# Local attention fused with two gated layers: the global queries' PV product issued inside the local PV block

## The chip, the cores and the metric

One core of one Trainium2 chip runs the whole program. The metric is device time in microseconds of one execution, the median of several.

## The reference

Attention with a local window and a few global tokens, then two token-wise layers. Batch 4, 8 heads of width 64, 32 global and 512 local tokens per batch, all in float32:

```python
k_all, v_all = concat([k_g, k_l]), concat([v_g, v_l])
out_g = softmax(scale * q_g @ k_all.T) @ v_all           # 32 global queries see all 544 keys
s_ll  = where(|i - j| <= 32, scale * q_l @ k_l.T, -1e9)
s_lg  = scale * q_l @ k_g.T
out_l = softmax(concat([s_lg, s_ll])) @ v_all            # local queries: window and global keys
x = concat([out_g, out_l]) as 2176 tokens x 512
x = rmsnorm(x) * rms_g
x = (silu(x @ w_gate) * (x @ w_val)) @ w_out             # first layer, width 1536
x = (s * relu(x @ w_in)**2 + b) @ w_out2                 # second layer, width 2048
```

## The kernel before, in words

The 2176 tokens go through the two layers in five groups: the local tokens of batches 0, 1 and 2 (512 each), and two groups of 320 with the halves of batch 3 and the global tokens. A group takes 12 slots of the first layer and 16 of the second. In a slot `emit_first` forms a 128-wide slice of hidden units in a PSUM bank `m` (two buffers), ACT and DVE apply the gate or the square, and `emit_second` adds the slice's product to four accumulators `acc` one slot later. Every product is three matmuls (lines 622, 623, 624), since each operand is split into a rounded part and a rest (`hl`, line 140: a cast on ACT or DVE, then a subtraction on DVE, line 142). Here they are called the large matmuls. In the first group the weights are also read from their raw form and converted on ACT and DVE (`conv`, lines 171 to 192); later groups load the converted ones.

The attention of the next group runs between the large matmuls. A unit is one batch and one pair of heads; `unit_steps` (line 290) gives its steps, `unit_queue` (line 410) strings those of four units together, and `tick` emits the next step when a modelled time allows: the distance is the step's lag or the time left divided by the steps left, whichever is longer, at most 4 us. The framework then orders each engine's instructions itself by a simulation, so a different queue changes the order of much besides the edit.

Steps of a unit with local queries: scores and their row maxima (`sc`, DVE line 281), exponentials (`st_e`, ACT line 331), reciprocals (`st_r`), scaling (`st_n`), transposes (`st_t`, PE lines 253 and 254, copied to SBUF on ACT line 257), and the local PV (`st_v`, line 386): `values` issues 16 matmuls on line 268 and 8 with the global keys on line 276, then DVE copies the result `u` (line 138) and the loads of the next unit are issued. All attention matmuls use one PSUM tile `at` of two banks with one buffer.

Odd units (`kp`) also do the global queries of their own and the preceding unit: scores (`st_g`, lines 318 and 319), one exponential, transposes (`st_tg`, lines 357 and 359, copied into `pgt`) and `st_gv`: 20 matmuls on line 377 into an `at` tile of their own, copied by DVE to `xg` (line 379). The trace counts each float32 matmul twice, as two passes. Six units have local queries and are odd; two more odd units have global queries only.

At the end of a group's second layer `build_steps` (line 444) makes the next group's input `x`: squares on ACT (455), a sum over partitions on PE (470), a logarithm and an exponential on ACT (474, 475, each with a table load), four DVE steps (476 to 479), and per slice a scaling (487) and a split into `x`.

Of the kernel before, what the change touches and what calls it, by code (L numbers as in the profile page):

```python
# [19 lines left out]
SG, SL = 32, 512  # L20
# [5 lines left out]
VW = 9 * 128 + 64  # L26
# [37 lines left out]
def attn_moe_kernel(ctx: ExitStack, tc: tile.TileContext, s0, q, k, v, w1, w2, cst, out):  # L64
# [27 lines left out]
    V, A, G, PE = nc.vector, nc.scalar, nc.gpsimd, nc.tensor  # L92

    def banks(tag):
        return ps.tile([128, 2, 512], F32, tag=tag, name=tag)
# [6 lines left out]
    def in_turn(mms):  # L102
        for a, b in zip(mms, mms[1:]):
            tc.add_manual_dep(b.ins, a.ins.name, behind, reason="in turn")
# [29 lines left out]
    def cpy(e, out_, in_):  # L134
        if e == "A":
            A.copy(out=out_, in_=in_)  # L136
        else:
            V.tensor_copy(out=out_, in_=in_)
# [68 lines left out]
    def u_tile(b):  # L207
        if b not in ut:
            ut[b] = u_p.tile([128, HP, 4, 128], F32, tag="u", name="u")
        return ut[b]  # L210

    def xg_tile(b):
        if b not in xg_t:
            xg_t[b] = xg_p.tile([128, HP, SG], F32, tag=f"xg{b}", name="xg")
        return xg_t[b]

    def load_u(i):
        if i >= len(UNITS) or i in raw_u:
            return
        b, p, loc = UNITS[i]  # L220
        vr = at_p.tile([128, VW], F32, tag="vr", name="vr", bufs=2)
        e = ST if loc else SG
        qr = at_p.tile([128, ST], F32, tag="qr", name="fq")
        kr = kr_p.tile([128, 8, KW], F32, tag="kr", name="fk")
        nc.sync.dma_start(out=qr[:, 0:e], in_=q[b, p, :, 0:e])
        nc.sync.dma_start(out=kr, in_=k[b, p])
        nc.sync.dma_start(out=vr, in_=v[b, p])
        raw_u[i] = (qr, kr, vr)
# [28 lines left out]
        A.copy(out=t.rearrange("p a n -> p (a n)"), in_=flat[:, 0:640])  # L257
        return t

    def values(bk, vr, vg, pts):  # L260
        mms = []
        for c in range(2 * len(pts)):
            t = pts[c // 2]
            for e in range(2):
                for h in range(2):
                    i = 2 * c + e
                    o = 128 * (c // 2) + 64 * e
                    mms.append(PE.matmul(bk[64 * h:64 * h + 64, c % 2, o:o + 64],  # L268
                                         lhsT=vr[:, 128 * i + 64 * h:128 * i + 64 * h + 64],
                                         rhs=t[:, 2 * (c % 2) + h, 64 * e:64 * e + 64], start=(c < 2 and e == 0), stop=False))  # L270
        for c in range(2 * len(pts)):
            t = pts[c // 2]
            for h in range(2):
                x = slice(32 * (2 * (c % 2) + h), 32 * (2 * (c % 2) + h) + 32)
                o = 128 * (c // 2)
                mms.append(PE.matmul(bk[64 * h:64 * h + 64, c % 2, o:o + 128], lhsT=vg[x], rhs=t[x, 4],
                                     start=False, stop=(c // 2 == len(pts) - 1), tile_position=(x.start, 64 * h)))
        in_turn(mms)
# [11 lines left out]
    def unit_steps(i):  # L290
        b, p, loc = UNITS[i]
        S = {}
        kp = p % 2
# [70 lines left out]
            A.copy(out=tv[:, 1:5], in_=bk[:, 1].rearrange("p (a n) -> p a n", a=4))  # L364
            S["pgt"] = t

        def st_gv():
            bk = banks("at")[:, 0]
            t = S["pgt"]
            mms = []  # L370
            for e in range(2):
                vr = raw_u[i - 1 + e][2]
                for a in range(5):
                    for h in range(2):
                        o = bk[64 * h:64 * h + 64, SG * e:SG * e + SG]
                        w = 128 * min(2 * a, 8) + 64 * h
                        mms.append(PE.matmul(o, lhsT=vr[:, w:w + 64], rhs=t[:, a, e, h], start=(a == 0), stop=(a == 4)))  # L377
            in_turn(mms)
            V.tensor_copy(out=xg_tile(b)[:, p - 1:p + 1], in_=bk[:, 0:2 * SG].rearrange("p (e n) -> p e n", e=2))
            if not loc:  # L380
                load_u(i + 1)

        def st_t(c0):
            S["pt", c0] = transposes(banks("at"), pm[:, c0:c0 + 2], S["gl", c0])

        def st_v():
            bk = banks("at")
            vr = raw_u[i][2]
            values(bk, vr, vr[:, VW - 64:VW], [S["pt", 0], S["pt", 2]])
            cpy("V", u_tile(b)[:, p].rearrange("p (c b) n -> p c b n", b=2),  # L390
                bk[:, :, 0:256].rearrange("p b (c n) -> p c b n", c=2))
            load_u(i + 1)

        if not loc:
# [7 lines left out]
            se=[(lambda: st_e((0, 1), False), 1.0)] + ([(st_g, 0.8)] if kp else [])  # L402
            + [(lambda: st_e((2, 3), kp == 1), 1.0)],
            rn=[(st_r, 1.0), (lambda: st_n(0), 0.3), (lambda: st_n(1), 0.3)]
            + ([(st_tg, 1.5), (st_gv, 1.0)] if kp else []),
            tv=[[(lambda: st_t(0), 1.0), (lambda: (st_n(2), st_n(3)), 1.0), (lambda: st_t(2), 1.0)]],
            pv=[[(st_v, 1.5)]])

# [255 lines left out]
    for n, (ph, gi, f) in enumerate(slots):  # L664
# [13 lines left out]
        w = wt[n]  # L678
        if ph == 1:
# [9 lines left out]
            h = act_p.tile([128, 2, NMAX], F32R, tag="h", name="h")  # L689
            a = tmp_p.tile([128, NMAX], F32, tag="ta", name="a")  # L690
# [8 lines left out]
        else:  # L699
# [7 lines left out]
            t = tmp_p.tile([128, NMAX], F32, tag="ta", name="t")  # L707
            h = act_p.tile([128, 2, NMAX], F32R, tag="h", name="h2")
# [93 lines left out]
```

## Time and profile before

| | |
|---|---|
| median of 3 runs | 996.24 us (994.8 to 998.65) |
| the profiled execution | 997.97 us |
| its span | 995.6 us |
| PE busy | 946.3 us, 95% of the span |
| DVE, ACT busy | 471.7 us, 464.9 us |
| mean granted TensorE clock | 0.972 of full speed |

The span runs from the first to the last instruction on the core. PE's busy time counts overlapping matmuls once, so gaps between its rows are what is left. A matmul's row is longer than the distance to the next one, since matmuls are pipelined; the cost of a stretch is read from the starts of its rows.

### The profile page before, as it was taken

What the parts mean: (1) busy time and instruction counts of PE and PEld (TensorE: products, weight loads), DVE (VectorE), ACT (ScalarE), POOL (GpSimd) and SP (SyncE); (2) the same over time, 40 slices, a digit from 0 to 9 for tenths busy, and PEclk for the clock granted to TensorE, in tenths of its full rate; (3) what the DMA queues carried; (4) which work ended last, traced back from release to release, by engine and by line L of the source; (5) the groups of instructions that cost most, each with busy time, mean ns of one, the idle gap of its engine ahead of it and who ended that gap; (6) DMA issues with size and microseconds to landing.
All of it is one profiled execution on the core that took longest, in us unless ns stands there. A gap on an engine that the chain in (4) does not pass through costs nothing.

```text
span 995.6 us, 15191 instructions
## 1 busy us (share of the span) xinstructions
PE 946.3 (95%) x6024; PEld 790.7 (79%) x6024; DVE 471.7 (47%) x1149; ACT 464.9 (47%) x908; POOL 0.8 (0%) x9
## 2 busy tenths in 40 slices
PE   5758999889999999999999999999999999999998
PEld 4437777667877778777877878778789999999998
DVE  6995978769954141334353131443442243421322
ACT  5886697667744152533346252633441342311222
POOL 0000000000000000000000000000000000000000
PEclk9578999999999999999999999999999999999999
DMA  9985789848964754446565655346488848988584
GB/s 371 409 324 204 282 306 349 308 162 311 356 240 170 264 203 183 163 143 225 213 232 191 239 204 187 142 173 245 167 308 337 305 159 309 340 338 300 181 328 153
DMA packets 41110, 249.54 MB, mean 251 GB/s; under 512 B 5072, under 2 KB 6096, under 8 KB 23120
## 3 DMA queue, kind: packets, MB, share of 16 engines
q1 hardware_dynamic: 41040, 248.58, 67.4%
q8 instruction: 47, 0.77, 0.3%
q14 instruction: 23, 0.19, 0.0%
HBM read 208.46 MB, written 40.11 MB: 250 GB/s over the span
## 4 chain that ended last, share of the span: by engine, by line
PE 80%; DMA 7%; DVE 6%; ACT 5%; issue 1%; SPq 0%; ACTq 0%; DVEq 0%
PE m L622 15%; PE m L624 14%; PE m L623 14%; PE acc L622 10%; PE acc L623 10%; PE acc L624 10%; DMA wr<-in_w_dram 4%; DMA wt<-wsc 2%; PE at L237 2%; PE at L268 1%; ACT ce L177 1%; PE at L377 1%; PE at L253 1%; DVE wt L142 1%; DMA fq<-in_q_dram 1%
## 5 line engine op out<-in xcount | busy, mean ns | idle before, releaser
L623 PE MATMUL acc<-h,wt 128*128 128x512 f32 (+1 forms) x560 | 200.6, 359 | 1.4 <-DVE h L142 1.3
L624 PE MATMUL acc<-h,wt 128*128 128x512 f32 (+1 forms) x560 | 200.2, 358 | 0.0
L622 PE MATMUL acc<-h,wt 128*128 128x512 f32 (+1 forms) x560 | 192.5, 363 | 0.5 <-DVE y L142 0.3
L622 PE MATMUL m<-x,wt 128*128 128x512 f32 (+2 forms) x496 | 178.7, 362 | 11.3 <-ACT x L136 9.2
L623 PE MATMUL m<-x,wt 128*128 128x512 f32 (+2 forms) x496 | 175.8, 355 | 0.1
L624 PE MATMUL m<-x,wt 128*128 128x512 f32 (+2 forms) x496 | 175.3, 354 | 0.0
L622 PE MATMUL m<-y,wt 128*128 128x512 f32 (+1 forms) x320 | 117.0, 373 | 7.6 <-DVE t L711 4.2
L623 PE MATMUL m<-y,wt 128*128 128x512 f32 (+1 forms) x320 | 116.2, 364 | 2.9 <-DVE y L142 2.9
L623 PEld LDWEIGHTS acc<-h,wt 128*128 128x128 f32 x560 | 105.2, 188 | 15.3 <-DVE h L142 2.1
L622 PEld LDWEIGHTS acc<-h,wt 128*128 128x128 f32 x560 | 103.6, 188 | 16.3 <-issue 1.7
L624 PEld LDWEIGHTS acc<-h,wt 128*128 128x128 f32 x560 | 105.1, 188 | 13.6 <-issue 0.5
L624 PE MATMUL m<-y,wt 128*128 128x512 f32 (+1 forms) x320 | 115.4, 361 | 0.0
L622 PEld LDWEIGHTS m<-x,wt 128*128 128x128 f32 x496 | 93.9, 190 | 26.4 <-ACT x L136 9.9
L692 DVE TENSOR_TENSOR a<-sg,m 128x512 f32<-128x512 f32 (+1 forms) x60 | 36.4, 607 | 142.9 <-PE m L624 136.5
L624 PEld LDWEIGHTS m<-x,wt 128*128 128x128 f32 x496 | 93.9, 189 | 11.1 <-issue 0.3
L623 PEld LDWEIGHTS m<-x,wt 128*128 128x128 f32 x496 | 93.9, 189 | 10.8 <-DVE x L142 0.8
L711 DVE SCALAR_TENSOR_TENSOR t<-m,ct,r 128x512 f32<-128x512 f32 (+1 forms) x80 | 53.2, 670 | 98.3 <-ACT r L710 98.1
L710 ACT ACTIVATE r<-m 128x512 f32<-128x512 f32 (+1 forms) x80 | 42.1, 532 | 115.2 <-PE m L624 115.0
L685 ACT ACTIVATE sg<-m 128x512 f32<-128x512 f32 (+1 forms) x60 | 32.0, 534 | 96.9 <-PE m L624 96.7
L136 ACT CAST h<-a 128x512 fp32r<-128x512 f32 (+1 forms) x60 | 33.3, 555 | 92.2 <-DVE a L692 73.2
L622 PEld LDWEIGHTS m<-y,wt 128*128 128x128 f32 x320 | 59.8, 189 | 20.8 <-ACT y L136 4.4
L713 ACT ACTIVATE h<-t,ct 128x512 fp32r<-128x512 f32 (+1 forms) x80 | 52.2, 658 | 50.9 <-DVE t L711 33.1
(141 smaller groups left out, 1137.6 us busy)
## 6 DMA issues: line engine op xcount, KB each, us to landing
wt<-wsc SPq DMA_DIRECT2D x48, 1536.0 KB, 7.5
wt<-wsc SPq DMA_DIRECT2D x64, 1024.0 KB, 4.8
wr<-in_w_dram SPq DMA_DIRECT2D x68, 512.0 KB, 6.3
wsc<-wt SPq DMA_DIRECT2D x12, 1536.0 KB, 7.3
wsc<-wt SPq DMA_DIRECT2D x16, 1024.0 KB, 6.2
fk<-in_k_dram SPq DMA_DIRECT2D x16, 640.0 KB, 5.3
vr<-in_v_dram SPq DMA_DIRECT2D x16, 608.0 KB, 6.0
s_w<-in_s_dram SPq DMA_DIRECT2D x8, 736.0 KB, 11.5
```

Of the source, the lines that this page charges most:

```text
L136: A.copy(out=out_, in_=in_)
L142: V.tensor_tensor(out=dst_l, in0=src, in1=dst_h.bitcast(F32), op=ALU.subtract)
L177: A.copy(out=e.bitcast(I16), in_=odd)
L237: mms.append(PE.matmul(bk[64 * e:64 * e + 64, h, n * KW:(n + 1) * KW], lhsT=qr[x, q0 + 64 * i:q0 + 64 * i + 64], rhs=kr[x, i]))
L622: PE.matmul(out_, lhsT=wh, rhs=xh, start=first, stop=False)
L623: PE.matmul(out_, lhsT=wh, rhs=xl, start=False, stop=False)
L624: PE.matmul(out_, lhsT=wl, rhs=xh, start=False, stop=last)
L685: A.activation(out=sg[:, :N], in_=gb[:, :N], func=AF.Silu)
L692: V.tensor_tensor(out=a[:, :N], in0=sg[:, :N], in1=vb[:, :N], op=ALU.mult)
L710: A.activation(out=r[:, :N], in_=hb[:, :N], func=AF.Relu)
L711: V.scalar_tensor_tensor(out=t[:, :N], in0=hb[:, :N], scalar=ct[:, C_S:C_S + 1], in1=r[:, :N], op0=ALU.mult, op1=ALU.mult)
L713: A.activation(out=h[:, 0, :N], in_=t[:, :N], func=AF.Identity, bias=ct[:, C_B:C_B + 1])
```

## The change

For odd units with local queries the step `st_gv` is gone from the queue. Its 20 matmuls are made by `gv_mms` and handed to `values`, which issues them between its matmuls with the local values (line 268) and those with the global keys. They write columns 256 to 319 of the first `at` bank, which the local PV leaves free, without start or stop flags. `gv_copy` then takes them to `xg`, ahead of the copy to `u`. Units with global queries only keep `st_gv`.

```diff
--- before.py
+++ after.py
@@ -257,7 +257,7 @@
         A.copy(out=t.rearrange("p a n -> p (a n)"), in_=flat[:, 0:640])
         return t
 
-    def values(bk, vr, vg, pts):
+    def values(bk, vr, vg, pts, more=None):
         mms = []
         for c in range(2 * len(pts)):
             t = pts[c // 2]
@@ -268,6 +268,8 @@
                     mms.append(PE.matmul(bk[64 * h:64 * h + 64, c % 2, o:o + 64],
                                          lhsT=vr[:, 128 * i + 64 * h:128 * i + 64 * h + 64],
                                          rhs=t[:, 2 * (c % 2) + h, 64 * e:64 * e + 64], start=(c < 2 and e == 0), stop=False))
+        if more:
+            mms += more()
         for c in range(2 * len(pts)):
             t = pts[c // 2]
             for h in range(2):
@@ -364,8 +366,7 @@
             A.copy(out=tv[:, 1:5], in_=bk[:, 1].rearrange("p (a n) -> p a n", a=4))
             S["pgt"] = t
 
-        def st_gv():
-            bk = banks("at")[:, 0]
+        def gv_mms(bk, fresh):
             t = S["pgt"]
             mms = []
             for e in range(2):
@@ -374,11 +375,18 @@
                     for h in range(2):
                         o = bk[64 * h:64 * h + 64, SG * e:SG * e + SG]
                         w = 128 * min(2 * a, 8) + 64 * h
-                        mms.append(PE.matmul(o, lhsT=vr[:, w:w + 64], rhs=t[:, a, e, h], start=(a == 0), stop=(a == 4)))
-            in_turn(mms)
+                        mms.append(PE.matmul(o, lhsT=vr[:, w:w + 64], rhs=t[:, a, e, h], start=(fresh and a == 0),
+                                             stop=(fresh and a == 4)))
+            return mms
+
+        def gv_copy(bk):
             V.tensor_copy(out=xg_tile(b)[:, p - 1:p + 1], in_=bk[:, 0:2 * SG].rearrange("p (e n) -> p e n", e=2))
-            if not loc:
-                load_u(i + 1)
+
+        def st_gv():
+            bk = banks("at")[:, 0]
+            in_turn(gv_mms(bk, True))
+            gv_copy(bk)
+            load_u(i + 1)
 
         def st_t(c0):
             S["pt", c0] = transposes(banks("at"), pm[:, c0:c0 + 2], S["gl", c0])
@@ -386,7 +394,10 @@
         def st_v():
             bk = banks("at")
             vr = raw_u[i][2]
-            values(bk, vr, vr[:, VW - 64:VW], [S["pt", 0], S["pt", 2]])
+            gk = bk[:, 0, 256:256 + 2 * SG]
+            values(bk, vr, vr[:, VW - 64:VW], [S["pt", 0], S["pt", 2]], (lambda: gv_mms(gk, False)) if kp else None)
+            if kp:
+                gv_copy(gk)
             cpy("V", u_tile(b)[:, p].rearrange("p (c b) n -> p c b n", b=2),
                 bk[:, :, 0:256].rearrange("p b (c n) -> p c b n", c=2))
             load_u(i + 1)
@@ -402,7 +413,7 @@
             se=[(lambda: st_e((0, 1), False), 1.0)] + ([(st_g, 0.8)] if kp else [])
             + [(lambda: st_e((2, 3), kp == 1), 1.0)],
             rn=[(st_r, 1.0), (lambda: st_n(0), 0.3), (lambda: st_n(1), 0.3)]
-            + ([(st_tg, 1.5), (st_gv, 1.0)] if kp else []),
+            + ([(st_tg, 1.5)] if kp else []),
             tv=[[(lambda: st_t(0), 1.0), (lambda: (st_n(2), st_n(3)), 1.0), (lambda: st_t(2), 1.0)]],
             pv=[[(st_v, 1.5)]])
```

**First place: PE, second unit of batch 1, in the first layer of the first token group.** Before, the global PV (377, 20 matmuls) and the local PV (268 and 276) are two blocks.

```order
L624 MATMUL acc_873<-h,wt 128x512
L377 MATMUL at<-pgt,vr 64x32 x20
L622 MATMUL m<-x,wt 128x512
...
L624 MATMUL acc_873<-h,wt 128x512
L268 MATMUL at<-ptf,vr 64x64 x16
L276 MATMUL at<-ptf,vr 64x128 x8
L622 MATMUL acc_872<-h,wt 128x512
```

Now (line numbers of the changed file: 378 is the global PV, 278 the old 276, 633 to 635 the old 622 to 624):

```order
L635 MATMUL m<-x,wt 128x512
L268 MATMUL at<-ptf,vr 64x64 x16
L378 MATMUL at<-pgt,vr 64x32 x20
L278 MATMUL at<-ptf,vr 64x128 x8
L633 MATMUL m<-x,wt 128x512
```

The 20 matmuls moved from a place of their own into the block of the local PV; all six units of this kind show the same.

**Second place: DVE, where the first group goes from its first to its second layer.** `y` is the second layer's input, in four slices of which the last two are in the rows; `qf` takes the next unit's global queries out of a load; `t` frees a bank for the second layer. `cv` and `wt` rows are weight conversion. Before:

```order
L142 TENSOR_TENSOR y<-acc_872,y 128x512
...
L187 SCALAR_TENSOR_TENSOR cv<-wr,cv 128x1024
L340 TENSOR_SCALAR rs<-sum 128x8
L300 COPY qf<-fq 64x32 x2
L189 SCALAR_TENSOR_TENSOR cv<-wr,cv 128x1024
L341 RECIPROCAL rs<-rs 128x8
L142 TENSOR_TENSOR y<-acc_873,y 128x512
L142 TENSOR_TENSOR wt<-cv,wt 128x2x512
...
L711 SCALAR_TENSOR_TENSOR t<-m,ct,r 128x512 x2
```

Now (line 722 is the old 711):

```order
L142 TENSOR_TENSOR y<-acc_872,y 128x512
L142 TENSOR_TENSOR y<-acc_873,y 128x512
L302 COPY qf<-fq 64x32 x2
L142 TENSOR_TENSOR wt<-cv,wt 128x2x512
L184 TENSOR_SCALAR cv<-cv 128x1024
L185 TENSOR_SCALAR cv<-cv 128x1024
L342 TENSOR_SCALAR rs<-sum 128x8
L187 SCALAR_TENSOR_TENSOR cv<-wr,cv 128x1024
L343 RECIPROCAL rs<-rs 128x8
L178 TENSOR_SCALAR cv<-cv 128x1024
L189 SCALAR_TENSOR_TENSOR cv<-wr,cv 128x1024
L722 SCALAR_TENSOR_TENSOR t<-m,ct,r 128x512
```

The last `y` moved ahead of `qf` and of a conversion; the first `t` now stands behind `qf`, the end of one conversion (142) and five steps of others (184, 185, 187, 178, 189).

**Third place: PE and DVE, where the first group gives way to the second.** Before, on PE, 15 large matmuls stand between the sum (470) and the next unit's first scores (237):

```order
L624 MATMUL acc_1926<-h_2625,wt 128x512
L470 MATMUL at<-ss,ones 128x512
L622 MATMUL acc_1926<-h_2625,wt 128x512
...
L624 MATMUL m<-y,wt 128x512
L237 MATMUL at<-fk,fq 64x160 x8
L622 MATMUL m<-y,wt 128x512
```

Now (481 is the old 470):

```order
L634 MATMUL m<-y,wt 128x512
L635 MATMUL m<-y,wt 128x512
L481 MATMUL at<-ss,ones 128x512
L237 MATMUL at<-fk,fq 64x160 x16
L633 MATMUL m<-y,wt 128x512
```

The sum now has no large matmul behind it, and both score blocks (16 matmuls) follow at once. On DVE, before, from the last step of the root (479) on:

```order
L479 SCALAR_TENSOR_TENSOR r_2654<-nt,r_2654 128x512
L487 SCALAR_TENSOR_TENSOR xn<-u,ct,r_2654 128x512
L711 SCALAR_TENSOR_TENSOR t<-m,ct,r 128x512
L281 ISA pm,nm<-at,ct 128x160
L281 ISA nm 128x1
```

Now (490 is the old 479, 498 the old 487, 283 the old 281):

```order
L490 SCALAR_TENSOR_TENSOR r_2652<-nt,r_2652 128x512
L283 ISA pm,nm<-at,ct 128x160
L283 ISA nm 128x1
...
L283 ISA pm,nm<-at,ct 128x160
L283 ISA nm 128x1
L498 SCALAR_TENSOR_TENSOR xn<-u,ct,r_2652 128x512
L722 SCALAR_TENSOR_TENSOR t<-m,ct,r 128x512
```

Four row maxima moved ahead of `xn` and `t`. On ACT a relu of the second `m` bank (710) moved ahead of the logarithm's table load (474). `t` frees the `m` bank that PE's next large matmul writes. The last local PV of batch 1 stands 29 large matmuls ahead of the sum before, and 22 now.

## Rows read from the trace of the kernel before

**Rows 1.** The page: busy time by engine, and the granted TensorE clock in 40 slices.
```profile
PE 946.3 (95%) x6024; PEld 790.7 (79%) x6024; DVE 471.7 (47%) x1149; ACT 464.9 (47%) x908; POOL 0.8 (0%) x9
...
PEclk9578999999999999999999999999999999999999
```

**Rows 2.** Timeline of PE around one global PV block (start us, us, instructions).
```profile
165.18 0.39 PE L624 MATMUL acc<-h,wt 128*128 128x512 f32 x1
...
165.86 0.39 PE L624 MATMUL acc<-h,wt 128*128 128x512 f32 x1
166.18 1.36 PE L377 MATMUL at<-pgt,vr 128*64 128x32 f32 x40
167.47 0.50 PE L622 MATMUL m<-x,wt 128*128 128x512 f32 x1
167.80 0.39 PE L623 MATMUL m<-x,wt 128*128 128x512 f32 x1
```

**Rows 3.** Groups by line on PE: count, busy us, mean ns, idle before.
```profile
L377 PE MATMUL at<-pgt,vr 128*64 128x32 f32 x320 | 11.6, 224 | 0.0
```

**Rows 4.** Instructions of line 379: duration ns min/median/max.
```profile
L379 DVE COPY xg<-at x8: 218/224/225, 170.1 to 808.1; 128x64 f32<-128x64 f32 x8
```

**Rows 5.** Timeline, first to second product of the first token group.
```profile
189.57 0.69 DVE L138 COPY u<-at 128x512 f32<-128x512 f32 x1
...
189.69 1.90 ACT L177 COPY ce<-wr 128x2048 int16<-128x2048 int16 x1 [2.57 <-DVE wt L142]
...
191.49 0.58 ACT L136 CAST y<-acc 128x512 fp32r<-128x512 f32 x1
...
196.73 1.28 ACT L331 ACT_TABLE_LOAD   x1
...
197.18 0.69 DVE L184 TENSOR_SCALAR cv<-cv 128x1024 f32<-128x1024 f32 x1
...
198.03 0.43 ACT L331 ACTIVATE pm<-pm,n 128x160 f32<-128x160 f32 x1
...
199.18 1.23 DVE L187 SCALAR_TENSOR_TENSOR cv<-wr,cv 128x1024 int32<-128x1024 int32 x1
...
202.45 0.37 DVE L300 COPY qf<-fq 64x32 f32<-64x32 f32 x2 [0.81 <-DMA fq<-in_q_dram]
...
204.10 0.64 DVE L142 TENSOR_TENSOR y<-acc,y 128x512 fp32r<-128x512 f32 x1
...
206.97 0.75 DVE L711 SCALAR_TENSOR_TENSOR t<-m,ct,r 128x512 f32<-128x512 f32 x1
```

**Rows 6.** Timeline, first to second token group.
```profile
279.96 0.50 PE L623 MATMUL acc<-h,wt 128*128 128x512 f32 x1
...
286.67 1.02 PE L470 MATMUL at<-ss,ones 128*128 128x512 f32 x2
...
287.73 0.69 ACT L474 ACTIVATE r<-at,epsc 128x512 f32<-128x512 f32 x1 [0.95 <-PE at L470]
...
288.44 1.28 ACT L475 ACT_TABLE_LOAD   x1
...
291.17 0.60 ACT L710 ACTIVATE r<-m 128x512 f32<-128x512 f32 x1 [0.81 <-PE m L624]
...
293.25 0.75 DVE L711 SCALAR_TENSOR_TENSOR t<-m,ct,r 128x512 f32<-128x512 f32 x1
...
293.91 0.32 DVE L281 CUSTOM_DVE_ANT_0 pm<-at,ct 128x160 f32<-128x160 f32 x1
...
294.14 0.66 PE L622 MATMUL m<-y,wt 128*128 128x512 f32 x1 [2.30 <-DVE t L711]
...
303.00 0.50 PE L622 MATMUL m<-x,wt 128*128 128x512 f32 x1 [0.64 <-DVE t L711]
```

**Rows 7.** Busy time by stretch: us, then PE, PEld, DVE, ACT, POOL busy (count), granted clock, DMA share, GB/s.
```profile
293.00:299.00 6.00, 4.86 (x14) 3.70 (x14) 4.62 (x15) 3.35 (x11) 0.00 (x0) 0.72 0.13 55
```

**Rows 8.** The page: DMA issues, KB each, median us from issue to landing.
```profile
vr<-in_v_dram SPq DMA_DIRECT2D x16, 608.0 KB, 6.0
```

## Prediction, made before the changed kernel was run

> **What bounds the kernel now.** I read the page first. PE is busy for 95% of the span and its granted clock is at 9 tenths or more from the fifth of 40 slices on [rows 1]; what can be won is PE's idle time or the work of a block, and this change removes no matmul. Then I went along the timeline of PE: after the start, which the change does not touch, its starts follow each other at the distance of a large matmul, except at two places. One is where the first token group goes from its first to its second layer. There ACT and DVE make the four slices of `y`, convert weights and serve a unit of attention at once [rows 5]. The other is where the first group gives way to the second: PE waits 2.30 us for a bank that `t` frees, behind the root of the norm [rows 6]. The later group changes have no such wait, since their weights are already converted. So the change can act in three ways: on the cost of a block itself, and on these two places, because the scheduler ordered everything anew.
>
> **The block.** Two large matmuls three apart start 0.68 us apart, 0.227 each. With the block of 40 passes between them, two neighbours start 1.61 us apart, and the one behind follows after 0.33 instead of 0.227 [rows 2]. So a block alone costs 1.61 - 0.227 + 0.10 = 1.48. From its first start to its last end it takes 1.36, of which a pass of its own length is 0.224 [rows 3], so a further pass adds (1.36 - 0.224) / 39 = 0.029 and forty cost 1.17 inside a running block. Saved: 0.31 for each of six units, **1.9 us**. This is all on PE and in the path. Ends: 0, if a change from line 268 to 377 and on to 276 costs what the ends of a block cost now, and 2.4, if a pass inside the block were 15% cheaper too.
>
> The copy to `xg` (0.22 us, [rows 4]) now stands ahead of `u` on DVE. The copy itself is not new; at five of the six units `u` has a unit's time until it is read, so I cost it at nothing there. At the sixth, see below. The `v` load that overwrites the preceding unit's values waits for the global PV, thus for the later block; a load lands after 6.0 us [rows 8] and its first reader is the local PV of the next unit, a whole unit's steps later. SP issues the loads in order, so what is queued behind a waiting `v` load waits too: converted or raw weights, which are asked for three slots ahead. I cost this at nothing; if the lead of three slots is used up, PE waits for the rest of a load, at most 6.0 us once. The shorter queue shifts the other steps of the first group by some matmuls; within dense PE work that costs nothing.
>
> **From the first to the second layer.** Before, from the start of the first `y` cast to the end of the last `y` on DVE is 204.10 + 0.64 - 191.49 = 13.25 us, and the first `t` ends at 207.72, 16.23 after that cast [rows 5]. With the new order ACT has four casts of 0.58, one conversion step of 1.90, the table load of 1.28 and four exponentials of 0.43, 7.2 in all, and then DVE's 0.64: the last `y` could be ready after 7.8. But the first `t` now stands on DVE behind `qf` (0.37), three steps of 1.23, three of 0.69, two short ones of together 0.36, and takes 0.75 itself: 7.24 more, so 15.1 against 16.23. That would gain 1.1. Against it, ahead of the first `y`: the rest `h` of the last slot now stands on DVE behind the copy to `xg`, `u` and a sum (0.22 + 0.69 + 0.69 = 1.6) that came after it before, and `y` needs `h`. I take **0**: the two nearly cancel. Lower end: 13.25 - 7.8 = 5.4 gained, if PE had only waited for `y`. Upper end: 3.6 lost; `qf` waits for a load and ended that wait 202.45 - 191.49 = 10.96 after the first cast. Were it as late again, `t` would end at 10.96 + 7.24 = 18.2, 2.0 later than before, and with the late `h` 3.6.
>
> **From the first to the second group.** Before, from the end of the last local PV of batch 1 (279.96) to the first matmul on the new `x` (303.00) is 23.04 us, with 68 large matmuls [rows 6]. In the new order this block stands 22 matmuls later, so 46 are left, and 23.04 - 22 x 0.227 = 18.05 would be no loss. Worked out anew: 22 matmuls to the sum with the exit of the block, 5.1. From the sum to the large matmul that waits for `t` it was 294.14 - 286.67 = 7.47, of which PE had work for most; now there are only the score blocks. To this chain the order adds on ACT a relu (0.60) and the table load (1.28), which stood ready before and now waits for the matmuls just ahead of the sum; the logarithm started 1.06 after the sum and would now start some 2.1 after it, 1.0 later. On DVE it adds four row maxima, at 0.32 at most 1.3, overlapped about 1.0. So 9.5. From there to the new `x`, 303.00 - 294.14 = 8.86 less the one score block that has moved ahead (1.0): 7.9. Sum 22.5, **4.4 lost**. PE's next matmuls run at a lower clock after that wait as they did before: 0.72 granted in the 6 us behind it [rows 7], between the levels of 1.2 and 2.4 GHz; this is inside the 8.86. Ends: 0, if the block in fact comes early enough that the root is done under it, and 6.1, if the low clock after the longer wait costs twice what these rows give (6 x 0.28 = 1.7).
>
> For this place one rule of the skill speaks against the change. The rows show that `u` is copied after the whole block and then takes 0.69 [rows 5]; with the global passes inside, the block ends 1.17 later and the copy to `xg` adds 0.22. The Trainium skill, "PSUM — Partial Sum Buffer", section "PSUM bank collisions raise a hardware error", asks to guard PSUM by bank and not by address, so finished columns of the same bank are not to be read while others are written. By it the 1.4 us stands wholly ahead of `u`. I count none of it: after the block come a copy, a square and a sum of about 0.69 each, a conversion step of 1.23 that may stand ahead, and 0.22, together 3.5, and the sum on PE comes 5.1 after the block. With the rule and no such slack the total would be 1.4 higher.
>
> **Sum:** -1.9 + 0 + 4.4 = +2.5 us. The profiled execution took 997.97 (span 995.6 and 2.4 around it), 1.7 above the median of 996.24. Against the median, the forecast is **998.7 us**.
>
> **Rivals.**
> - *The query load is late* (slower). At the first place `t` waits for `qf`, and `qf` for its load. Everything behind `qf` on DVE waits, now five conversion steps and `t`; before it was the last `y`. Price 3.6 instead of 0: -1.9 + 3.6 + 4.4 = +6.1, 1002.3. It decides from a `qf` 9.9 us after the first `y` cast on (16.23 + 2.5 - 1.6 - 7.24); it was 10.96. For it: DVE waited for this load. Against it: both score blocks, after which that load may start, come sooner in the new order. Chance 0.18.
> - *PE gets the early `y` in full, and the second place costs nothing* (faster): -1.9 - 5.4 = -7.3, 988.9. For it: PE's longest wait at the first place was for the last `y`. Against it: `t` is next in line. Chance 0.10.
> - *The change does not do what it says*: the ends of the block are saved, but the two changes of tile form inside it cost as much. 0 + 4.4: 1000.6. For it: 377 and 276 use different row counts. Against it: 268 and 377 have the same form. Chance 0.10.
> - *The slack under `u` is gone*, the rule above: +2.5 + 1.4, 1000.1. Against it the 1.6 us of slack worked out above. Chance 0.10.
>
> **Numbers.** The forecast has the rest, 0.52. A measurement of this kernel tells 0.5% from no change, 5 us: faster is below 991.3, slower above 1001.2. The forecast's own spread puts 0.40 of its 0.52 inside, 0.09 above, 0.03 below. The first rival puts 0.15 above and 0.03 inside; the second 0.09 below, 0.01 inside; the third and fourth 0.07 and 0.08 inside, 0.03 and 0.02 above. Faster 0.12, same 0.59, slower 0.29. The range is 992.0 to 1003.5: it leaves out most of the second rival and the far ends of the costs.
>
> **What would show it.** In the profile after: six blocks of 32, 40 and 16 passes in a row and no block of line 377's successor alone before batch 0's global units; each with one pair of slow starts around it in place of two, so 1.5 us less at the old place and 1.2 more at the new one. At the first place the last `y` well under 13 us after the first, and the PE wait for it replaced by one for `t`. At the second place a PE wait of 5 to 7 us ahead of the large matmul that `t` releases, instead of 2.30, and a low granted clock behind it. I am wrong if either place shows no wait on PE, if PE waits for weights or `v` after the first group, or if PE's large matmuls change their spacing elsewhere.

## The result, and the profile after

The changed kernel takes 1003.6 us (median of 6 runs, 1000.7 to 1005.87), the one before 995.4 beside it (6 runs, 994.58 to 998.65): ratio 1.0082, 95% interval 1.0065 to 1.0098. It is 0.8% slower, 4.9 us above the forecast and 0.1 above the range. The profiled execution after took 1003.17 us, its span 1001.4. Against the profiled execution before this is 5.2 more and not 8.2, since that one lay 2.6 above its median and the one after 0.4 below. The one before holds 1.9 us of PE waits for weights in its fourth token group; the one after has 1.0 of them, at the fifth group's `x` (871.86):

```profile
PE m L622 <- DMA wt<-wsc: 1.9, 2, 1.0
```

(PE's waits before, 733 to 870 us: sum, count, longest.) The page after, engines and granted clock, answers to [rows 1]:

```profile
PE 944.1 (94%) x6024; PEld 790.4 (79%) x6024; DVE 471.1 (47%) x1149; ACT 465.2 (46%) x908; POOL 0.8 (0%) x9
...
PEclk9678999999989999999999999999999999999999
```

PE is busy 2.2 us less than before, and the span is 5.8 longer. So 8 us in which PE is not busy are new. A table of marks shows where. A mark is the first large matmul on a group's `y` or on the next group's `x`; each column is the time between two marks, as a difference from the trace before, in us. All kernels of the experiments, which come below, stand in it. Each row is one execution; that of e1 lay 3.4 above its median.

| kernel | start to first y | to 2nd group's x | to its y | to 3rd group's x | to its y | to 4th group's x | sum |
|---|---|---|---|---|---|---|---|
| the change | -1.91 | +4.25 | +0.17 | +0.87 | +1.07 | +2.42 | +6.87 |
| e1 dummy step | -1.07 | +4.71 | +0.95 | +2.68 | +0.93 | +3.46 | +11.66 |
| e2 short queue | -0.84 | +5.95 | -1.73 | +2.62 | -0.77 | +2.79 | +8.02 |
| e3 merge b1 | -2.25 | +6.65 | -0.91 | 0.00 | +0.01 | -0.01 | +3.49 |
| e4 merge b2, b3 | -0.51 | -0.72 | +1.10 | +0.85 | +1.07 | +0.85 | +2.64 |
| e5 placeholder b2, b3 | -0.02 | +0.08 | +1.32 | +0.24 | +1.30 | +0.25 | +3.17 |
| e6 both blocks b2, b3 | +0.54 | +0.09 | +1.61 | +1.32 | +1.58 | +1.33 | +6.47 |
| e7 early end | +3.75 | -1.83 | -0.87 | +0.86 | +1.07 | +0.83 | +3.81 |
| e8 before, early end | +4.15 | -1.59 | +0.79 | -0.02 | +0.01 | -0.01 | +3.33 |
| e9 sum back | -1.94 | +4.70 | -0.32 | +0.86 | +1.08 | +0.85 | +5.23 |
| e10 layer change shift | -1.45 | +5.17 | -1.76 | +0.93 | -0.06 | +1.27 | +4.10 |
| e11 sum back and placeholder | -1.23 | +4.67 | -0.89 | +0.25 | +0.52 | +0.23 | +3.55 |
| e12 order held | -0.23 | -0.54 | -0.01 | +0.07 | 0.00 | +0.04 | -0.67 |
| e13 same, not held | -0.83 | +3.54 | -1.81 | +2.62 | 0.00 | +2.68 | +6.20 |
| e14 two pacings, 0.90 | +4.35 | -2.69 | -2.29 | +1.10 | -0.35 | +1.22 | +1.34 |
| e15 two pacings, 0.91 | +2.12 | -1.61 | -2.15 | +0.83 | -0.06 | +1.24 | +0.37 |

e3 to e6 and e12 share stretches of order with before, and differ there by up to 0.7. Where the granted clock differs, it can be more: e3 has PE's blocks where the change has them up to the second group's `x`, and its second column is 2.4 higher; of the two, e3 has the lower clock at the first layer change (0.56 granted from 205 to 212 us, 0.76 in the change). So a difference of 2 us in one of the first two columns says little by itself.

**The block.** PE's timeline after, around the last merged block of batch 1 (start us, us; answers to [rows 2]):

```profile
281.18 0.39 PE L634 MATMUL m<-y,wt 128*128 128x512 f32 x1
281.50 1.15 PE L268 MATMUL at<-ptf,vr 128*64 128x64 f32 x32
282.48 1.31 PE L378 MATMUL at<-pgt,vr 128*64 128x32 f32 x40
283.72 0.67 PE L278 MATMUL at<-ptf,vr 32*64 32x128 f32 x16
284.32 0.50 PE L633 MATMUL acc<-h,wt 128*128 128x512 f32 x1
```

The same local block before, alone (the matmul behind it, at 279.96, is in [rows 6]):

```profile
277.96 0.39 PE L623 MATMUL m<-y,wt 128*128 128x512 f32 x1
278.28 1.15 PE L268 MATMUL at<-ptf,vr 128*64 128x64 f32 x32
279.36 0.67 PE L276 MATMUL at<-ptf,vr 32*64 32x128 f32 x16
```

From neighbour to neighbour it is 3.14 us now and was 2.00, so the forty passes cost 1.14 inside, where the prediction read 1.48 for them alone: 0.34 saved per unit.

**First layer change.** Timeline after, answers to [rows 5]:

```profile
189.57 0.59 ACT L136 CAST y<-acc 128x512 fp32r<-128x512 f32 x1 [0.62 <-PE acc L635]
...
196.20 1.29 DVE L142 TENSOR_TENSOR y<-acc,y 128x512 fp32r<-128x512 f32 x2 [0.55 <-ACT y L136]
...
198.57 0.36 DVE L302 COPY qf<-fq 64x32 f32<-64x32 f32 x2 [1.08 <-DMA fq<-in_q_dram]
...
203.37 1.22 DVE L189 SCALAR_TENSOR_TENSOR cv<-wr,cv 128x1024 int32<-128x1024 int32 x1
...
204.50 0.74 DVE L722 SCALAR_TENSOR_TENSOR t<-m,ct,r 128x512 f32<-128x512 f32 x1
...
205.31 0.80 PE L633 MATMUL m<-y,wt 128*128 128x512 f32 x1 [4.45 <-DVE t L722]
```

The last `y` ends 7.9 us after the first cast (13.25 before), and PE then waits 4.45 us for the first `t`, which ends 15.7 after that cast (16.23 before).

**First to second group.** Timeline after, answers to [rows 6]:

```profile
289.44 1.02 PE L481 MATMUL at<-ss,ones 128*128 128x512 f32 x2
...
293.08 0.77 PE L237 MATMUL at<-fk,fq 64*64 64x160 f32 x16 [2.61 <-DVE msq L487]
...
296.33 0.32 DVE L283 CUSTOM_DVE_ANT_0 pm<-at,ct 128x160 f32<-128x160 f32 x1
...
297.54 1.35 PE L237 MATMUL at<-fk,fq 64*64 64x160 f32 x16 [3.69 <-DVE nm L283]
...
305.34 0.39 PE L633 MATMUL m<-x,wt 128*128 128x512 f32 x1
```

Two waits stand here in place of the one of 2.30. The first score block waits until DVE and ACT have read the sum out of `at`; the second until DVE has taken the first's row maxima out of the same tile, and those stand on DVE behind the root.

**Later layer changes.** Here is what the forecast did not look at. Timeline after, second group, ACT, DVE and PE:

```profile
416.50 1.28 ACT L333 ACT_TABLE_LOAD   x1
...
418.86 0.69 DVE L142 TENSOR_TENSOR h<-a,h 128x512 fp32r<-128x512 f32 x1 [1.66 <-ACT h L136]
419.46 0.32 DVE L283 CUSTOM_DVE_ANT_0 pm<-at,ct 128x160 f32<-128x160 f32 x1
...
420.76 0.43 ACT L333 ACTIVATE pm<-pm,n 128x160 f32<-128x160 f32 x1 [1.94 <-DVE n L330]
...
422.43 1.04 ACT L136 CAST y<-acc 128x512 fp32r<-128x512 f32 x2
...
423.04 0.73 PE L633 MATMUL m<-y,wt 128*128 128x512 f32 x2 [1.65 <-ACT y L136]
```

And the same place before:

```profile
416.07 0.33 DVE L281 CUSTOM_DVE_ANT_0 pm<-at,ct 128x160 f32<-128x160 f32 x1
...
416.78 1.28 ACT L331 ACT_TABLE_LOAD   x1
...
418.07 0.43 ACT L331 ACTIVATE pm<-pm,n 128x160 f32<-128x160 f32 x1
...
419.89 1.07 ACT L136 CAST y<-acc 128x512 fp32r<-128x512 f32 x2
...
420.53 0.73 PE L622 MATMUL m<-y,wt 128*128 128x512 f32 x2 [0.22 <-ACT y L136]
```

In both, the `y` casts stand on ACT behind four exponentials of the attention, these behind four row maxima on DVE, these behind a score block on PE. Before, that chain ended with PE: 0.22 us of wait, no slack. Now the row maxima stand behind the slot's `h`, and PE waits 1.65. It is so again in the third group.

**Within dense PE work.** The fourth and sixth columns of the change hold no PE wait above 0.15 us, and are longer all the same (the sixth by a low clock too, see the end). One score block of 16 passes, which went to PE as a whole before, now goes in three pieces with large matmuls between them (second group; before, then after):

```profile
440.78 0.39 PE L624 MATMUL m<-y,wt 128*128 128x512 f32 x1
441.09 0.77 PE L237 MATMUL at<-fk,fq 64*64 64x160 f32 x16
441.80 0.50 PE L622 MATMUL m<-y,wt 128*128 128x512 f32 x1
```

```profile
444.48 0.50 PE L237 MATMUL at<-fk,fq 64*64 64x160 f32 x6
444.91 0.73 PE L633 MATMUL acc<-h,wt 128*128 128x512 f32 x2
445.57 0.49 PE L237 MATMUL at<-fk,fq 64*64 64x160 f32 x4
...
447.81 0.50 PE L237 MATMUL at<-fk,fq 64*64 64x160 f32 x6
```

Before, the block lies between large matmuls that start at 440.78 and 442.13, two starts apart; the pieces lie between 444.16 and 448.57, eleven starts apart. Less 0.227 for each start, the block costs 0.90 and the pieces 1.91: 1.0 us more for two cuts. The third group has the same three pieces. Of the other kernels e4, e7, e9 and e13 have three pieces at both places, and e3, e5, e8, e10 to e12, e14 and e15 the whole block.

### The profile page after: what moved, and what is told of

It is laid out like the page before. It is cut to its first block, busy times and chain, and to the rows that moved or that the text cites. A ratio compares the mean times of both kernels' runs of the same rounds, so it can differ in the third digit from the quotient of the medians.

```text
span 1001.4 us, 15200 instructions
## 1 busy us (share of the span) xinstructions
PE 944.1 (94%) x6024; PEld 790.4 (79%) x6024; DVE 471.1 (47%) x1149; ACT 465.2 (46%) x908; POOL 0.8 (0%) x9
## 4 chain that ended last, share of the span: by engine, by line
PE 76%; ACT 10%; DVE 8%; DMA 5%; issue 1%; SPq 0%; ACTq 0%; DVEq 0%
PE m L633 14%; PE m L634 13%; PE m L635 13%; PE acc L633 10%; PE acc L635 9%; PE acc L634 9%; DMA wr<-in_w_dram 4%; ACT ce L177 2%; ACT pm L333 2%; ACT cv L176 1%; PE at L237 1%; PE at L268 1%; PE at L253 1%; DVE cv L187 1%; DVE pm L283 1%
## 5 line engine op out<-in xcount | busy, mean ns | idle before, releaser
L725 DVE SCALAR_TENSOR_TENSOR h<-t,ct,h 128x512 fp32r<-128x512 f32 (+1 forms) x80 | 53.5, 670 | 47.6 <-ACT h L724 47.2
```

What stands on the lines that cost most here:

```text
L725: V.scalar_tensor_tensor(out=h[:, 1, :N], in0=t[:, :N], scalar=ct[:, C_B:C_B + 1], in1=h[:, 0, :N].bitcast(F32), op0=ALU.add, op1=ALU.subt ...
```

## Experiments

**Theory A:** the merged block is cheap; the loss comes from the other order that the shorter queue gives. **Theory B:** the merged block itself costs (shared bank, later copies, later `v` loads).

### e1, e2: queue and block taken apart

e1 keeps the merge and puts a step that does nothing in the place of `st_gv`; e2 keeps the two blocks and drops the step.

```diff
-            + ([(st_tg, 1.5)] if kp else []),
+            + ([(st_tg, 1.5), (lambda: None, 1.0)] if kp else []),
```

```diff
-            + ([(st_tg, 1.5), (st_gv, 1.0)] if kp else []),
+            + ([(st_tg, 1.5)] if kp else []),
...
         def st_v():
+            if kp:
+                st_gv()
             bk = banks("at")
```

> The merged block stays, but a step that does nothing keeps the place and the lag of the removed step in the queue of the six units. Theory A (the merge itself is cheap, the loss comes from the other order that the shorter queue gives): the sum that ends the first group's norm stands 11 large matmuls later than before instead of 15, with the last local PV 10 later; that costs about 10 x 0.227 = 2.3 us, the six blocks give back 1.9, and the waits for y of 1.65 us at the layer changes of groups two and three fall below 0.6, since the exponentials come 17 large matmuls earlier. In all 995.8 us, 993 to 998, at least 5 below the change. Theory B (the merged block itself costs, by its shared bank, the later copy of u or the later v loads): 1002 to 1005, as the change.

> The two blocks stay apart as before, each in its own tile, but the global one has no step of its own: it is issued in the step of the local PV, right ahead of it. Theory A: no saving of 0.3 us per block, and the queue is as short as in the change; the last local PV of the first group now has no large matmul between it and the sum, so PE's wait there grows by 3 to 5 us over the change. 1007.5 us, 1004 to 1011, slower than the change. Theory B: with the blocks apart the time is that of before, 995.4, at most 998.

e1: 1003.82 us, ratio 1.0068 (1.0055 to 1.0081). e2: 1004.29, 1.0074 (1.0062 to 1.0086). Theory A's forecast for e1 was 8 too low; that for e2 was 3 too high, with the result just inside its range, and Theory B's was 9 too low. e2, which has no merged block at all, loses as much as the change: B is not needed for the loss. e1 shows that the queue's length alone doesn't set the order: the removed step also claimed the one `at` tile, and without that the score blocks of the second layers come up to 45 large matmuls earlier than before. New waits follow, such as this one (PE's waits of e1, 405 to 440 us) for the scaled scores, which stand behind exponentials:

```profile
PE at L253 <- DVE pm L290: 1.1, 1, 1.1
```

### e3, e4: which units

```diff
-            + ([(st_tg, 1.5)] if kp else []),
+            + ([(st_tg, 1.5)] + ([] if b == 1 else [(st_gv, 1.0)]) if kp else []),
...
-            if kp:
+            if kp and b == 1:
                 gv_copy(gk)
```

e4 has `b > 1` in place of `b == 1`.

> The change in the two odd units of batch 1 alone; batches 2 and 3 keep their own step and tile. Theory A: the first group goes as in the change and everything behind it as before; before plus 2.3 (the difference of the first matmul on the second group's x in the two traces): 997.7 us, 996 to 999.5, with PE waits for the root behind the sum, and no wait over 0.4 us for y at later layer changes. Theory B: two of six blocks, a third of the 8.2 us: 998.1, but spread over the two units, with no wait behind the sum above before's 2.30.

> The change in the four odd units of batches 2 and 3 alone. Theory A: up to the second group's x as before; then the waits for y of 1.65 us each at two layer changes and the half clock behind one of them, less 4 x 0.31: before plus 3.4 (the rest of the difference of the two traces), 998.8 us, 997 to 1000.5. Theory B: four of six blocks, two thirds of 8.2: 1000.9. Theory C (the layer changes cost only their two waits less the four blocks, and the rest of the difference is spread between executions): 2 x 1.43 - 1.2 = 1.7, 997.1.

e3: 999.57, 1.0027 (1.0016 to 1.0038). e4: 1001.77, 1.0046 (1.0031 to 1.0061). Against 996.81 for the kernel before beside them, the two parts add up to 7.7 us, nearly the whole 8.2. The table shows the places: e3 loses all of it between the first `y` and the second group's `x` and nothing later; e4 nothing there, and about 1 at each of four marks: two waits for `y`, and two score blocks in three pieces. Both came out above all their forecasts, and by the totals alone A and B could not be told apart here.

### e5, e6: the order held in batches 2 and 3

The removed step stays as one matmul into its own `at` tile (e5), or as the whole separate block with its copy (e6), beside the merged one.

```diff
+        def st_hold():
+            bk = banks("at")[:, 0]
+            PE.matmul(bk[0:64, 0:SG], lhsT=raw_u[i - 1][2][:, 0:64], rhs=S["pgt"][:, 0, 0, 0])
...
-            + ([(st_tg, 1.5)] if kp else []),
+            + ([(st_tg, 1.5), (st_hold if b > 1 else st_gv, 1.0)] if kp else []),
```

> The four odd units of batches 2 and 3 are merged as in the change, but their removed step stays as one matmul of two passes into an attention tile of its own, whose result nobody reads. That holds the scheduler's order: ACT has exactly the order of before, PE and DVE differ by a few places. Theory A (the merged block is cheap, the order costs): a block alone cost 1.48, two passes alone some 0.35, forty passes inside 1.17, so 4 x 0.04, nothing: 996.8 us, 995.5 to 998.5, with no wait over 0.4 us for y at the later layer changes. Theory B (the merged block costs 1.2 us a unit, as the four units of the run without the holder did): 1001 to 1002.5.

> As the last run, but the held step makes the whole separate block and its copy too, so that the four units compute the global PV twice. The order is that of before but for the merged block. What it takes longer than before is the price of forty passes and one copy inside the local block, nothing else: Theory A 4 x 1.17 = 4.7, 1001.5 us (1000.5 to 1002.5). If a further pass in the shared bank were dearer, or the copy of u stood in the way (Theory B, 1.2 more a unit): 1006.3.

e5: 999.29, 1.0029 (1.0016 to 1.0041). e6: 1002.62, 1.0063 (1.0043 to 1.0082). Large matmul by large matmul, e5 gains 1.07 us at each old place and loses 1.13 at each new one, and e6 loses 1.13 at each new one: the merged passes cost what the block's rows said. What is left is at the layer changes, 1.4 each in e5 and 0.7 in e6. So e5 lies between the ranges of both theories, and e6 0.1 above that of A. In e5 ACT's order is that of before; on DVE alone four row maxima moved ahead of the slot's product `a` (line 708 there), which came at 415.41 before (e5's timeline):

```profile
416.00 0.33 DVE L283 CUSTOM_DVE_ANT_0 pm<-at,ct 128x160 f32<-128x160 f32 x1 [5.10 <-PE at L237]
...
416.98 0.68 DVE L708 TENSOR_TENSOR a<-sg,m 128x512 f32<-128x512 f32 x1
417.70 0.62 ACT L136 CAST h<-a 128x512 fp32r<-128x512 f32 x1 [2.99 <-DVE a L708]
```

With that the `h` cast, the table load and the exponentials behind it come 1.6 us later, and the `y` casts 1.4 (421.29 against 419.89). The forecast of no new wait was wrong, its prices were right.

### e7, e8: the first group ends earlier

```diff
-            sched["end"] = sched["t"] + 0.95 * tot
+            sched["end"] = sched["t"] + (0.95 if gi else 0.9) * tot
```

> The change, with the first group's steps paced to end earlier (0.90 of the modelled time in place of 0.95): the last local PV of batch 1 now has 31 large matmuls between it and the sum, and 51 behind the sum before the second group's x, in place of 22 and 0 (before: 29 and 15). Theory A: the wait behind the sum goes, 5 to 6.5 us less than the change; the first layer change is ordered anew and may give or take 2: 997.6 us, 994.5 to 1000.5. Theory B: the place behind the sum does not matter, 1003.6.

> The same pacing of the first group in the kernel before, blocks apart. 37 large matmuls between the last local PV and the sum and 36 behind it. Theory A: the waits of 2.30 and 0.64 us there and the low clock behind go, 3.5 us less than before, with 2 either way from the first layer change: 993 us, 990.5 to 996. Theory B: no difference, 996.8.

e7: 998.96, 1.0029 (1.0016 to 1.0042), in the range of A, but not by A's reason. The wait behind the sum is gone, and between the first `y` and the second group's `x` it is 6.1 us shorter than the change; but ahead of the first `y` it is 5.7 longer, with a new PE wait of 3.9 for `h`. Up to the second group's `x` that leaves 0.4 of the 4.1 us between the two profiled spans. The rest came later, 1.6 of it in the sixth column, where the change alone had a low clock. e8: 999.65, 1.0043 (1.0031 to 1.0056), 3.9 slower than before where 3.5 faster was expected: the blocks apart, the order changed, and a loss is there, ahead of the first `y`.

### e9, e10, e11: the two places mended in the change

```diff
+        if ph == 2 and f == 0 and gi == 0:
+            sched["end"] -= 3.0
```

e10 adds `(0.97 if gi else 0.95) * tot`, e11 to e9 the placeholder of e5.

> The change, with the modelled end of the first group 3 us earlier from its second layer on. That puts the sum at the first group change back to where it was before: 30 large matmuls behind the last local PV and 15 ahead of the next group's x (the change: 22 and 0; before: 29 and 15). The first layer of the first group, its layer change and the four units of batches 2 and 3 keep the order of the change. Theory A (what that place lost is the missing cover behind the sum): the 4.25 us that the two traces differ there come back: 999.3 us, 997.5 to 1000.5. Theory B (the place of the sum does not matter; the loss comes with the merged blocks): 1003.6.

> The last kernel, with the later groups' steps paced a little slower (0.97 for 0.95). On ACT the first y cast of these groups then stands ahead of the second set of four exponentials instead of behind it. Theory A (the later layer changes lose because y stands behind exponentials that wait for their row maxima): PE's two waits for the first y, 1.65 us each, go, and the half clock behind one of them; the second y still stands behind four exponentials, so up to 1 us of each stays: 2 less than the last kernel, 997.3 us, 995.5 to 999. Theory B (other costs of the layer change): no difference from the last kernel.

> The kernel with the sum back, and in the four units of batches 2 and 3 the one placeholder matmul that held the order of before. Theory A: at the later layer changes what the placeholder won before, 1001.8 to 999.3, so 2.5 less than the kernel with the sum back: 996.8 us, 995 to 998.5. With the blocks' saving it should be no slower than before. Theory B: the placeholder's win was due to something else in that kernel, no difference: 999.3.

e9: 1002.15, 1.0060 (1.0045 to 1.0074): 1.4 less than the change by the medians, where A had said 4.3. e10: 1000.35, 1.0043 (1.0029 to 1.0058). e11: 998.86, 1.0028 (1.0017 to 1.0039). The sum of e9 stands where it stood before, but its second score block still stands right behind the first, while 14 large matmuls lay between them before. PE's waits of e9, 280 to 308 us:

```profile
PE at L237 <- DVE nm L283: 3.3, 1, 3.3
PE m L633 <- DVE t L724: 0.6, 1, 0.6
```

So two causes share this place: the missing cover behind the sum (the wait of 2.61, gone here) and the second score block (3.69, now 3.27). From the matmul behind the last local PV of batch 1 to the new `x`, e9 takes 24.87 us for 69 large matmuls; by the rows of before (23.04 for 68) it loses 1.6 there, and the change 3.0. The second column shows nothing of this, since ahead of that PV e9 loses 1.8 more than the change, 0.9 of it in a longer wait for `t` (1.21 against 0.33). e10 and e11 won 1.8 and 3.3 over e9 by their medians, where A had said 2 and 2.5; in the columns of the layer changes, the third to the sixth, it is 2.1 and 2.4.

### e12, e13: the same merged blocks, with and without the old order

Merged are only the second odd units of batches 1 to 3. e12 has the placeholder, e13 has not.

```diff
-            + ([(st_tg, 1.5)] if kp else []),
+            + ([(st_tg, 1.5), (st_hold if p == 3 else st_gv, 1.0)] if kp else []),
...
-            if kp:
+            if kp and p == 3:
                 gv_copy(gk)
```

> Merged in three units only, the second odd unit of each batch (heads 6 and 7), each with the one placeholder matmul. ACT's order is that of before to the last row; on PE the score blocks stand where they stood, on DVE the row maxima too, and only the copy to xg has moved. Theory A (merged block cheap, order costs): 3 x 0.06 (what block and placeholder together came to per unit in the placeholder run: 1.07 less at the old place, 1.13 more at the new one), no new wait: 996.1 us, 995 to 997.5, and ratio under 1.0015. Theory B (1.2 us a merged unit, whatever the order): 999.5.

> The same three merged units without the placeholder, so with three steps fewer in the queues and another order: the sum of the first group 12 large matmuls later, the second score block right behind the first there, and at the later layer changes a y cast ahead of the second set of exponentials. Theory A: 3 x 0.31 saved, and some 4 us lost behind the sum and 1 to 2 at the layer changes: 1000 us, 998 to 1003, at least 2 above the run with the placeholder. Theory B: the same as the run with the placeholder, less the 3 x 0.35 of the placeholders.

e12: 996.49, 1.0003 (0.9988 to 1.0019): the time of before. e13: 1001.83, 1.0059 (1.0039 to 1.0079). The merged blocks are the same three; e13 even has the three placeholders less. The order, with the waits and pieces that come with it, makes 5.3 us; e13 has a PE wait of about 1.1 us for `y` at each of the two later layer changes, and the pieces. PE's waits from 300 to 740 us, which hold the two later layer changes, of before, the change, e5 and e12:

```profile
PE m L622 <- ACT y L136: 0.4, 2, 0.2
```

```profile
PE m L633 <- ACT y L136: 3.3, 2, 1.7
```

```profile
PE m L638 <- ACT y L136: 1.7, 2, 0.9
```

```profile
PE m L638 <- ACT y L136: 0.4, 2, 0.2
```

And e12 from 280 to 308 us, where before has the same row with the same numbers:

```profile
PE m L638 <- DVE t L727: 2.9, 2, 2.3
```

This settles it for these three units: in the order of before the merged blocks and their placeholders cost nothing that can be measured (the interval reaches from 0.1% below to 0.2% above), and neither layer changes nor the group change lose. All six units merged in the order of before were not run; in e5, with four, DVE's order had moved.

### e14, e15: the full change, paced anew

Both pace the later groups to 0.97; the first to 0.90 (e14) and 0.91 (e15).

```diff
-            sched["end"] = sched["t"] + 0.95 * tot
+            sched["end"] = sched["t"] + (0.97 if gi else 0.9) * tot
```

> The full change with both shifts that won something alone: the first group paced to 0.90, the later ones to 0.97, no placeholder. If the two places add up: 998.96 for the first alone, less 1.8 (the second alone, 1002.15 to 1000.35): 997.2 us, 995.5 to 999. If they do not (the pacing only moves the loss on): 999 to 1000.

> As the kernel with both pacing shifts, but the first group paced to 0.91 for 0.90. On ACT the last casts of h of the first layer then stand ahead of the exponentials and their table load, where 0.90 had one behind two sets of them, for which PE waited 4.60 us. Behind the sum the order stays (33 large matmuls ahead of it, 49 behind). Theory A: most of that wait goes, a part comes back as a wait for y, which now has exponentials ahead of it in two places: 3 less than that kernel, 994.3 us, 992.5 to 997, as fast as before or a little faster. Rival: the first layer change only trades one wait for another, 997.3.

e14: 997.31, 1.0011 (0.9997 to 1.0025); by the total the two shifts add up as forecast. PE's longest wait there is at the first layer change (183 to 212 us):

```profile
PE acc L633 <- ACT h L136: 4.6, 1, 4.6
```

e15 puts that cast of `h` ahead of the exponentials: 996.72, 1.0010 (1.0001 to 1.0019). The wait is gone, but PE waits 1.74 us for row maxima and 2.56 for the first `y` there, and the ratio is that of e14, so the rival held: the first layer change trades one wait for another. So the full change can be brought to within 0.1% of before; no version here is faster than before.

## Why the prediction was wrong

**The block** (-1.9): right. 0.34 for each of six units is 2.0. The rival that the change of forms inside the block eats the saving is out by these rows, and e12 leaves little room for a cost beside it.

**First to second layer** (0): right as a number, and by luck. The last `y` was forecast 7.8 after the first cast and came at 7.9; the first `t` 15.1, and it came at 15.7. The price of 1.6 for a late `h` did not come: the stretch ahead of the first `y` became 1.91 shorter, by a block's 0.34 and by waits for `h`, `u` and the first `y` that were 2.9 in sum before (1.4 now, 1.2 of it for the gate `sg`). And no gain came behind the first `y`: up to the last local PV of batch 1 the change loses 1.3, or 1.6 without a block's 0.34, with PE waiting 4.45 for `t`. So a gain ahead and a loss behind cancel, where the forecast had a loss ahead and a gain behind. The rival of the late query load did not decide: `qf` came 9.0 after the first cast, ahead of the 9.9 from which it would have, but DVE did wait 1.08 for that load with `t` behind it.

**First to second group** (+4.4): right in sign, too high by 1.4. From the matmul behind the last local PV of batch 1 (284.32) to the new `x` (305.34) it took 21.02 us; 22.5 was forecast, and 18.05 would have been no loss, so 3.0 were lost. That the table has +4.25 here is no hit, since 1.3 of it lie at the first layer change. The 5.1 us to the sum and the 9.5 from there to the large matmul that `t` releases came as forecast (5.1, and 9.4 to 298.87). The rest took 6.5 and not 7.9: the wait of 0.64 at its end is gone, and half of the low clock fell under the second wait (granted 0.51 from 294 to 301 us, with PE waiting until 297.54), so that it did not cost twice what it had cost before, as the upper end had it. The place of the wait was not as forecast: not 5 to 7 us ahead of the large matmul that `t` releases, but 2.61 and 3.69 ahead of the two score blocks. Four row maxima were priced at 1.0 on DVE; that PE's second score block needs the tile that they empty was not seen, and e9, where the cover is back, still loses 1.6 of the 3.0: about half. The rule on PSUM banks (the Trainium skill, "PSUM — Partial Sum Buffer", section "PSUM bank collisions raise a hardware error") changed nothing, as forecast: `u` was copied after the whole block, at 284.60, its sum of squares ended at 286.67, and PE's sum stood at 289.44 behind large matmuls.

**The step that failed** is the sentence that the later group changes have no such wait, with the one that a shift within dense PE work costs nothing. Of the group changes the first is true; the layer changes of the later groups were not looked at, and the second is false. Behind the second group's `x` the traces differ by 0.17 + 0.87 + 1.07 + 2.42 = 4.5 us up to the fourth group's `x`, where four merged blocks should have given back 4 x 0.34 = 1.4. So 5.9 us went unseen. 2.9 are the two waits for `y` at the layer changes of the second and third group, 1.65 in place of 0.22 each; 2.0 are the two score blocks in pieces, within dense PE work; 1.6 are the low clock behind the second wait, in this one execution. Ahead of the second group's `y` a local PV in three pieces in place of five gives about 0.9 back, and 0.3 are open. The trace of before had the sign of the waits: PE waited 0.22 us for `y` at both places. These waits were passed over, and they meant that a chain through PE, DVE and ACT ended exactly with PE, so that a delay of it goes into PE's time. These 5.9 are as much as the whole difference of the two spans, 5.8: the blocks' 2.0 and 1.1 in the fourth group (0.9 of it waits for weights) pay for the 3.0 of the group change.

**Which time to add to.** The rows of the sum come from one execution, and the range was for medians. A forecast that had hit the 5.2 between the two profiled executions would still have fallen 3 short of the 8.2 between the medians; 0.9 of it are the weight waits that the one had and the other had not.

## What to carry to other kernels

An edit that takes a step out of a modelled queue is two changes: the cheaper block, and a new order of everything behind it. Price them apart, and try them apart: a placeholder that claims the same tile for one matmul held the order in e12, and nearly in e5, and showed the block's own price. In the trace, look for the waits of 0.2 us as well as for the long ones: they mark chains without slack, and an order found by a simulation moves such chains by microseconds. And count the pieces into which each block of small matmuls is cut: no wait shows them.

## What the runs showed of the hardware

The same wait cost differently in two places. At the layer changes of the second and third group the change has a PE wait of 1.65 us for `y`; behind the first the granted clock stayed full, behind the second it fell (the stretches 423 to 429 and 640 to 646 us: us, PE, PEld, DVE, ACT, POOL busy, granted clock, DMA share, GB/s):

```profile
423.00:429.00 6.00, 5.96 (x27) 4.55 (x28) 3.85 (x10) 3.52 (x8) 0.00 (x0) 1.00 0.35 108
640.00:646.00 6.00, 5.43 (x18) 4.00 (x18) 3.54 (x11) 3.46 (x9) 0.00 (x0) 0.72 0.28 119
```

0.72 lies between the levels of 1.2 and 2.4 GHz. In e4 and e9, with the same order and the same wait, the third group's second layer lost 0.85 and not 2.42, so this cost 1.6 us in the one execution. At the first group change it is the same: PE waits 2.3 us for `t` in the kernel before and in e12; the 6 us around its end had 0.72 granted before [rows 7], and the full clock in e12:

```profile
294.00:300.00 6.00, 5.06 (x34) 3.87 (x35) 5.26 (x22) 4.20 (x13) 0.00 (x0) 1.00 0.11 45
```

In these traces a short idle time of PE has no fixed price: it may or may not take the clock with it.
